# An attention and two-MLP kernel on one core: queues planned with another matmul cost, another rule for transfers, and unit tiles in groups of 4, 4, 8

## The chip, the core and the metric

One core of a Trainium2 chip runs the whole program. The metric is device time in microseconds (us). The engines are PE (matrix products), DVE (vector), ACT (activations), POOL (a second, slower vector engine) and SP, which only issues transfers. Each runs its own queue of instructions strictly in order and waits on semaphores where an operand is not ready.

## What is computed

A chunked attention (24 chunks of 32 queries, each against 56 neighbouring keys and 8 memory keys), then a first MLP whose activation is a rational function, then a second, gated MLP with four experts:

```python
# attention, per chunk: softmax(scale * q_c @ k_full.T) @ v_full
x = attn_out.transpose(0, 2, 1, 3).reshape(1536, 512)
# first MLP, w_in 512x2048, w_out 2048x512
h = x @ w_in
g = (a0 + a1*h + a2*h**2 + a3*h**3) / (1 + |b0|*|h| + |b1|*h**2 + 1e-6)
x = g @ w_out
# second MLP, E = 4 experts, w1 512x1024, w2 1024x512 each
out = sum_e p[:, e] * (relu(x @ w1[e]) @ w2[e])
```

## The kernel before

**Blocks and units.** The 1536 tokens are three blocks of 512. Attention is cut into 24 units (8 per block), each of 256 tokens and two heads. A unit has three pieces of PE work: the scores (L427, with a mask at L424), the transposes of the probabilities (L462), and the values (L479). Between them stand its softmax on DVE, POOL and ACT (L433 to L456) and the copies of the probabilities (L282). Its result goes to a tile of `x` (L548, L553).

**Splits.** Products run on pairs of a rounded value and its remainder, three products for each exact one (`PAIRS`). So everything that PE reads is split first: ACT copies the rounded half (L281), POOL or DVE subtracts to get the rest (L326).

**Steps of the first MLP.** The hidden size 2048 is cut into 16 unit tiles of 128. A step is one unit tile on one block, so there are 48 steps, numbered 0 to 47. I write A(i) for the first product of step i (12 matmuls, L569, into a bank of `h` or `att`) and B(i) for its second product (12 matmuls, L681, added up in the four `acc` banks). On PE, B(i) follows A(i+3) (`LAG` = 3). Between A(i) and B(i) stands the chain of the activation: ACT L633, L635, L672, L673; DVE L638, L642, then three instructions at L650, the last of which writes `ts<-ts,h` or `ts<-ts,att`; POOL L669; then ACT L281 and POOL L326, which write the split `g`. DVE has five instructions of this chain per step.

**Weights of the first MLP.** Each unit tile of weights comes as 64-bit words in two halves: half 0 for A, half 1 for B. A half is loaded (L349), converted by three DVE instructions (L352, L358, L364, here called a conversion), copied by ACT (L281) and split by POOL (L326, `w<-y,w`). Tiles live in the 10 buffers of `w`, which also hold the units' operands.

**Groups.** `GS = 4, 4, 4, 4` says that four unit tiles are run over all blocks before the next four, the blocks forward and backward in turn. This gives nine segments (block, first tile, end tile): (0,0,4) (1,0,4) (2,0,8) (1,4,8) (0,4,12) (1,8,12) (2,8,16) (1,12,16) (0,12,16). A segment ends after steps 3, 7, 15, 19, 27, 31, 39, 43 and 47. At its end the four `acc` banks are evicted: by ACT for the first segment of a block, by four DVE additions at L700 for the six others. The next segment's first B needs the freed banks.

**Second MLP.** Chunks of two unit tiles: direct products (L569), products on sums and differences of tiles (L795), second products (L928) evicted by DVE (L943, L945). The sums over blocks (`plan_sums_x`, L726) need two blocks to be finished.

**What sets the order.** All work is given to a planner as operations with costs (`Plan.add`), and `Plan.run` simulates the engines with those costs and emits the instructions in the order in which they came out. `MM` is the cost of one matmul of 512 columns, 0.2325. `Op.at` gives the moment at which an operation may start: its forerunners' ends plus a lag. Nominal PE times come from `tick`, which adds up costs in the order of the loops. Where the plan shows PE idle for over `FGAP`, `fill` adds matmuls on zeros (L294). These costs decide the order alone; on the chip every instruction waits for its real operands.

Of the kernel before, what the change touches and what calls it, by code (L numbers as in the profile page):

```python
# [26 lines left out]
NQ = 4  # L27
# [59 lines left out]
class Op:  # L87
# [4 lines left out]
        self.start = self.end = self.eng = None  # L92

    def at(self, e):
        return max((a.end + Plan.lag(a.eng, e) for a in self.after), default=0.0)


class Plan:
# [50 lines left out]
    def run(self):  # L149
        for o in self.ops:  # L150
            o.wait = len(o.after)
            o.start = o.end = None
            o.ready = 0.0
            for b in o.bufs:
                b.left, b.free = len(b.users), None
        live = {t: [] for t in BUFS}
        slots = {t: [] for t in BUFS}
        turn = {t: [] for t in BUFS}
        for o in sorted(self.ops, key=lambda o: (o.alap, o.n), reverse=True):
            for b in reversed(o.takes):  # L160
# [12 lines left out]
        for o in self.ops:  # L173
            if not o.wait:
                offer(o)
        done = 0
        while done < len(self.ops):
            best = None
            for e, lst in can.items():
                pick = None  # L180
                for o, c in lst:
                    if o.start is not None:
                        continue
                    t = max(free[e], o.at(e))
# [3 lines left out]
                    for b in o.takes:  # L188
                        if b.tag in live:
                            if turn[b.tag][-1] is not b:  # L190
# [3 lines left out]
                            if len(occ) >= BUFS[b.tag]:  # L194
                                times = sorted(x.free if x.free is not None else 1e9 for x in occ)
                                x = times[len(occ) - BUFS[b.tag]]
                                if x >= 1e9:
                                    ok = False
                                    break
                                t = max(t, x + 0.2)  # L200
                    if not ok:
                        continue
                    k = (t, o.alap)
                    if pick is None or k < pick[0]:
                        pick = (k, t, o, c)
                if pick is not None:
                    can[e] = [x for x in lst if x[0].start is None]
                    if best is None or pick[1] < best[0]:
# [43 lines left out]
def emit(ctx: ExitStack, tc: tile.TileContext, qk, v0, kv, q8, w64, w32, coef, prob, out):  # L252
# [140 lines left out]
    class Unit:  # L393
# [11 lines left out]
        def plan(self, t_scores, t_trans, t_values):  # L405
            u, blk, hp = self.u, self.blk, self.hp


            T = Buf("w", [128, 2048], F32)
            st = Buf("st", [128, 8], F32)  # L410
            P1, P2, P3 = self.psum_buf(), self.psum_buf(), self.psum_buf()
# [7 lines left out]
            def scores():  # L419
# [1 line left out]
                r = (blk * (BLK // UT) + self.half) % UPB  # L421
                edge = {0: 0, UPB - 1: NQ - 1}.get(r)
                if edge is not None:
                    PE.matmul(P1.ap[:, wide(edge)], ident_h, mask[:, min(edge, 1)], start=True, stop=False)  # L424
                for n in sorted(range(NQ), key=lambda n: n != edge):
                    for c in range(2):
                        PE.matmul(  # L427
                            P1.ap[64 * c : 64 * c + 64, wide(n)], q(c * NQ + n), k(c * NQ + n),
                            start=(n != edge), stop=True,
                        )  # L430

            def peaks():
                DVE.tensor_reduce(  # L433
                    out=nm(), in_=P1.ap[:, : NQ * KB].rearrange("p (n k) -> p n k", n=NQ),
                    axis=AX.X, op=ALU.max, negate=True,
                )

# [3 lines left out]
            def exps():  # L441
                for n in range(NQ):
                    ACT.activation(
                        k(n), P1.ap[:, n * KB : (n + 1) * KB], AF.Exp, scale=SCALE,
                        bias=nm()[:, n : n + 1], accum_out=sm()[:, n : n + 1],
                    )

# [12 lines left out]
            def trans():  # L460
                for n in range(2):
                    PE.transpose(  # L462
                        P2.ap[:, n * 128 : n * 128 + 128], T.ap[:, n * 128 : n * 128 + 128], ident
                    )

            def probs(j):
# [1 line left out]
                r = slice(64 * j, 64 * j + 64)  # L468
                copy(o_probs[j].eng)(
                    T.ap[r, 1024:1536].rearrange("p (g t x) -> p g t x", t=2, x=CH)[:, :, j],  # L470
                    P2.ap[r, :UT].rearrange("p (g x) -> p g x", x=CH),
                )

            def values():
                for n in range(2):
                    for c in range(2):
                        for h in range(2):
                            j = n * 4 + c * 2 + h
                            PE.matmul(  # L479
                                P3.ap[64 * h : 64 * h + 64, wide(c * 2 + n)],  # L480
                                v()[:, wide(j)], q(j), start=True, stop=True,
                            )

# [43 lines left out]
            o = add(  # L527
                [("POOL", 0.65)], norm3, [o], [st, T]
            )
            o2 = add([("PE", 0.22)], trans, [o], [T], [P2], key=t_trans)  # L530
            o_probs = [
                add(
                    [("ACT", 0.39), ("DVE", 0.45)] if blk == 0 else [("ACT", 0.39)],
# [1 line left out]
                )  # L535
                for j in range(2)
            ]
            o3 = add([("PE", 0.62)], values, [*o_probs, lv], [T], [P3], key=t_values)
            if u == FU:
                plan_warm(1, [o3], t_values + 0.1)  # L540
            ps = lambda: P3.ap[:, :UT]
            c = slice(self.half * UT, (self.half + 1) * UT)
            first = self.half == 0
            if first:
# [10 lines left out]
                ),  # L555
                [hi], [P3, X],
            )


    part, x2, acc, o_t = {}, {}, {}, {}  # L560
# [423 lines left out]

    todo = {}
    for b in range(1, NBLK):
        n = 2 * GS[0]
        for j in range(UB):
            at = b * n - UEND - (UB - 1 - j) * n / UB
            for part_, d in ((2, U2), (1, U1), (0, 0)):  # L990
                todo.setdefault(max(-1, round(at + d)), []).append((-part_, UB * b + j, part_))
    cost = (0.7, 0.22, 0.62)

    def attend(slot):
        for _, u, part_ in sorted(todo.pop(slot, [])):
            ut[u, part_] = tick(cost[part_])

    attend(-1)
    swaps = (GS[0], 2 * GS[0])
# [189 lines left out]
```

## Time and profile before

| what | value |
|---|---|
| time, median of 3 runs | 843.77 us (842.98 to 843.96) |
| the profiled execution | 843.32 us, of which its span is 841.5 us |
| PE busy | 819.9 us (97%) |
| DVE / POOL / ACT busy | 623.6 / 381.1 / 356.5 us |
| the chain that ended last | PE 65%, DVE 21%, ACT 5%, POOL 4%, DMA 2% |

A busy share counts an instruction as busy from its start to its (modelled) end, and a matmul that is held back can look long instead of late. So the distance from one start to the next tells more than the share. Times in the rows below count from the start of the span. "Idle before" is the time in which the engine stood still ahead of an instruction, with what ended the wait.

### The profile page before, as it was taken

What the parts mean: (1) busy time and instruction counts of PE and PEld (TensorE: products, weight loads), DVE (VectorE), ACT (ScalarE), POOL (GpSimd) and SP (SyncE); (2) the same over time, 40 slices, a digit from 0 to 9 for tenths busy, and PEclk for the clock granted to TensorE, in tenths of its full rate; (3) what the DMA queues carried; (4) which work ended last, traced back from release to release, by engine and by line L of the source; (5) the groups of instructions that cost most, each with busy time, mean ns of one, the idle gap of its engine ahead of it and who ended that gap; (6) DMA issues with size and microseconds to landing.
All of it is one profiled execution on the core that took longest, in us unless ns stands there. A gap on an engine that the chain in (4) does not pass through costs nothing.

```text
span 841.5 us, 11342 instructions
## 1 busy us (share of the span) xinstructions
PE 819.9 (97%) x4214; PEld 664.9 (79%) x4218; DVE 623.6 (74%) x929; ACT 356.5 (42%) x783; POOL 381.1 (45%) x350
## 2 busy tenths in 40 slices
PE   7889999999899998999999999999999999999998
PEld 4667778778788886788888888888888888888886
DVE  6988799999996679965766766766766765765754
ACT  6798886767666666430321321320320330330310
POOL 4797777877777797640321320330330330330300
PEclk9999999999999999999999999999999999999999
DMA  9976122212210100000101101101101101100003
GB/s 349 357 268 211 51 76 76 76 67 85 75 51 23 31 0 26 26 27 24 51 1 50 51 1 50 51 1 51 51 1 51 50 4 48 51 12 13 1 1 150
DMA packets 21911, 55.41 MB, mean 66 GB/s; under 512 B 3936, under 2 KB 3936, under 8 KB 21856
## 3 DMA queue, kind: packets, MB, share of 16 engines
q1 hardware_dynamic: 21856, 54.69, 19.0%
q8 instruction: 33, 0.54, 0.3%
q14 instruction: 22, 0.18, 0.1%
HBM read 51.54 MB, written 3.15 MB: 65 GB/s over the span
## 4 chain that ended last, share of the span: by engine, by line
PE 65%; DVE 21%; ACT 5%; POOL 4%; issue 2%; DMA 2%; SPq 0%; DVEq 0%; ACTq 0%; POOLq 0%
PE acc L928 30%; PE att L569 10%; PE h L795 10%; PE att L795 7%; DVE ts L650 5%; PE h L569 3%; PE acc L681 3%; DVE tm L638 2%; DVE tm L642 2%; DVE p L700 2%; DVE y L358 2%; DVE y L352 1%; DVE att L650 1%; DVE y L364 1%; DMA w<-kv 1%
## 5 line engine op out<-in xcount | busy, mean ns | idle before, releaser
L326 POOL TENSOR_TENSOR w<-stg,w 128x512 fp32r<-128x512 f32 x64 | 96.3, 1513 | 314.5 <-ACT w L281 314.5
L945 DVE SCALAR_TENSOR_TENSOR p<-acc,pr,p 128x512 f32<-128x512 f32 x180 | 135.2, 751 | 100.5 <-PE acc L928 100.5
L928 PE MATMUL acc<-w,g 128*128 128x512 f32 x768 | 177.5, 390 | 0.7 <-DVE p L943 0.6
L928 PEld LDWEIGHTS acc<-w,g 128*128 128x128 f32 x768 | 143.9, 188 | 31.6 <-DVE p L943 1.5
L681 PE MATMUL acc<-g,w 128*128 128x512 f32 x576 | 146.2, 398 | 4.1 <-DVE p L700 3.0
L569 PE MATMUL att<-x,w 128*128 128x512 f32 x624 | 147.8, 390 | 1.7 <-DVE ts L650 1.7
L569 PEld LDWEIGHTS att<-x,w 128*128 128x128 f32 x624 | 117.1, 188 | 26.3 <-DVE ts L650 2.1
L681 PEld LDWEIGHTS acc<-g,w 128*128 128x128 f32 x576 | 107.9, 190 | 31.2 <-DVE p L700 4.5
L281 ACT ACTIVATE ts<-h 128x512 f32<-128x512 f32 x15 | 9.0, 598 | 239.1 <-PE h L795 239.1
L569 PE MATMUL h<-x,w 128*128 128x512 f32 x384 | 96.5, 396 | 1.0 <-DVE ts L650 0.8
L928 PE MATMUL acc<-w,gb 128*128 128x512 f32 x384 | 89.6, 389 | 0.0
L569 PEld LDWEIGHTS h<-x,w 128*128 128x128 f32 x384 | 70.7, 188 | 16.8 <-DVE ts L650 1.3
L928 PEld LDWEIGHTS acc<-w,gb 128*128 128x128 f32 x384 | 72.1, 188 | 14.9
L326 POOL TENSOR_TENSOR g<-ts,g 128x512 fp32r<-128x512 f32 x48 | 66.7, 1390 | 26.7 <-ACT g L281 26.3
L669 POOL TENSOR_TENSOR ts<-ts,tu 128x512 f32<-128x512 f32 x48 | 63.8, 1329 | 12.8 <-ACT ts L658 10.9
L326 POOL TENSOR_TENSOR w<-y,w 128x512 fp32r<-128x512 f32 x36 | 49.9, 1386 | 8.3 <-ACT w L281 8.0
L281 ACT ACTIVATE g<-ts 128x512 fp32r<-128x512 f32 x48 | 30.3, 631 | 39.7 <-DVE ts L650 39.6
L795 PE MATMUL h<-x,w 128*128 128x512 f32 x180 | 45.7, 389 | 0.0
L795 PE MATMUL att<-x,w 128*128 128x512 f32 x180 | 45.7, 389 | 0.0
L795 PE MATMUL h<-w 128*128 128x512 f32 x180 | 45.7, 389 | 0.0
L795 PEld LDWEIGHTS h<-x,w 128*128 128x128 f32 x180 | 33.8, 188 | 7.0
L795 PEld LDWEIGHTS att<-x,w 128*128 128x128 f32 x180 | 33.8, 188 | 7.0
(122 smaller groups left out, 1168.3 us busy)
## 6 DMA issues: line engine op xcount, KB each, us to landing
stg<-w SPq DMA_DIRECT2D x64, 512.0 KB, 3.5
w<-kv SPq DMA_DIRECT2D x32, 256.0 KB, 5.2
w<-q SPq DMA_DIRECT2D x16, 256.0 KB, 4.8
w<-qk SPq DMA_DIRECT2D x8, 400.0 KB, 6.3
out<-p SPq DMA_DIRECT2D x12, 256.0 KB, 2.0
w<-v SPq DMA_DIRECT2D x8, 256.0 KB, 6.7
pr<-prob SPq DMA_DIRECT2D x1, 24.0 KB, 3.7
cf<-coef SPq DMA_DIRECT2D x1, 3.0 KB, 6.0
```

The costliest lines, as they stand in the source:

```text
L281: return lambda o, i: ACT.activation(o, i, AF.Copy)
L326: engines[op.eng].tensor_tensor(out=dst[:, 1], in0=src, in1=dst[:, 0].bitcast(F32), op=ALU.subtract)
L358: DVE.scalar_tensor_tensor(out=y.ap, in0=words(1), scalar=-(1 << 30), in1=y.ap, op0=ALU.bitwise_and, op1=ALU.bitwise_or,)
L569: PE.matmul(s.h.ap, wt[w].ap[:, 0, a, k * 128 : (k + 1) * 128], xs[k].ap[:, b], start=(k == 0 and n == 0), stop=(k == KT - 1 and n == 2),)
L638: [("DVE", 0.6)], lambda: DVE.tensor_tensor(out=m.ap, in0=m.ap, in1=h.ap, op=ALU.mult), [li], [h, m]
L642: lambda: DVE.scalar_tensor_tensor(out=m.ap, in0=m.ap, scalar=A1, in1=h.ap, op0=ALU.add, op1=ALU.mult),
L650: lambda: DVE.scalar_tensor_tensor(out=out.ap, in0=in0.ap, scalar=scalar, in1=in1.ap, op0=op0, op1=op1),
L669: lambda: POOL.tensor_tensor(out=s.ap, in0=s.ap, in1=u.ap, op=ALU.mult), [ln], [s, u],
L681: PE.matmul(ps, wt[f].ap[:, 1, a, d * 128 : (d + 1) * 128], g.ap[:, b], start=start, stop=stop)
L795: PE.matmul(ps.ap, left(a, k), right(b, k), start=k == 0 and n == 0, stop=k == 1 and n == 2,)
L928: PE.matmul(ps.ap, gs[j][0].ap[:, a, d * 128 : d * 128 + 128], wt[f].ap[:, 1, b], start=j == 0 and n == 0, stop=j == 1 and n == 2,)
L945: DVE.scalar_tensor_tensor(out=y, in0=ps.ap, scalar=p, in1=y, op0=ALU.mult, op1=ALU.add)
```

## The change

- `MM` becomes 0.2267. The costs of the attention's PE pieces become 0.85, 0.25 and 0.8 (`PARTS`; before 0.75, 0.22 and 0.62).
- In the plan, an SP operation that follows another SP operation may start 0.5 after the other's start (`Op.at`); before, it waited for the landing and a lag of 0.9. So a unit's `v` may be issued right behind its keys and queries.
- `GS` becomes 4, 4, 8. The segments are (0,0,4) (1,0,4) (2,0,8) (1,4,8) (0,4,16) (1,8,16) (2,8,16): seven, ending after steps 3, 7, 15, 19, 31, 39 and 47. The last blocks to end now come in the order 0, 1, 2 (before 2, 1, 0), so block 0 is finished after step 31.
- Attention pieces are planned as generators; PSUM banks of units 8 to 11 are taken in the order of the pieces. Merging pieces into one PE operation is written down, but `MERGED` = 9 is beyond the last block, so nothing is merged.

```diff
-MM = 0.2325
+MM = 0.2267
-UEND, U1, U2 = 3, 2, 3
+UEND, UD, MERGED = 3, (0, 2, 3), 9
+PARTS, GROUPED, SWITCH = (0.85, 0.25, 0.8), (0.5, 0.22, 0.45), 0.3
-GS = 4, 4, 4, 4
+GS = 4, 4, 8
     def at(self, e):
-        return max((a.end + Plan.lag(a.eng, e) for a in self.after), default=0.0)
+        return max((a.start + 0.5 if a.eng == e == "SP" else a.end + Plan.lag(a.eng, e) for a in self.after), default=0.0)
...
-            o1 = add([("PE", 0.75)], scores, [*ready, o_mask, o_ident], [T], [P1], key=t_scores)
+            o1 = yield 0, scores, [*ready, o_mask, o_ident], [T]
+            P1 = self.at[0][0]
...
+    def cost_of(parts):
+        return PARTS[parts[0]] if len(parts) == 1 else SWITCH + sum(GROUPED[n] for n in parts)
+
+    def attend_ops(wants, key):
...
+        o = add([("PE", cost_of([w[2][0] for w in wants]))], go, after, uses, takes, key=key)
+        return [gen.send(o) for _, gen, _ in wants]
...
-    for u in units:
-        u.plan(*(ut[u.u, j] for j in range(3)))
+    for u in units[:UB]:
+        gen = u.parts()
+        want = next(gen)
+        for j in range(3):
+            (want,) = attend_ops([(u, gen, want)], ut[u.u, j])
+    gens, wants = {u.u: u.parts() for u in units[UB:]}, {}
```

**First place: SP at the start of the program.** `qk` and `v` are the operands of the units of block 0, `kv` and `q` those of later units, `stg` a half of a weight tile of the first MLP. Before:

```order
L502 DMA w<-qk 128x800 x7
L509 DMA w<-v 128x512
L502 DMA w<-qk 128x800
L509 DMA w<-v 128x512
L349 DMA stg<-w 128x512
L509 DMA w<-v 128x512
L505 DMA w<-kv 128x512
L506 DMA w<-q 128x512
L509 DMA w<-v 128x512
```

After, from the same place:

```order
L508 DMA w<-qk 128x800 x5
L515 DMA w<-v 128x512
L508 DMA w<-qk 128x800
L515 DMA w<-v 128x512
L508 DMA w<-qk 128x800 x2
L515 DMA w<-v 128x512 x6
L351 DMA stg<-w 128x512
L511 DMA w<-kv 128x512
L512 DMA w<-q 128x512
```

All eight `v` of block 0 now stand ahead of the first weight half; before, six of them stood behind it, with later units' operands and two more weight halves in between. For later units, too, `v` now follows its keys: the `v` of units 10 and 11 stood behind five weight halves (tiles 0 to 3, and half 1 of tile 0) and now stand behind three.

**Second place: DVE after step 27.** `y<-stg` are conversions, `tm`, `h`, `att` and `ts` belong to the chain of steps 27 to 29, `p<-acc,p` is an eviction. Before:

```order
L650 SCALAR_TENSOR_TENSOR ts<-ts,h 128x512
L638 TENSOR_TENSOR tm<-tm,h 128x512
L642 SCALAR_TENSOR_TENSOR tm<-tm,cf,h 128x512
L364 SCALAR_TENSOR_TENSOR y<-stg,y 128x512
L352 TENSOR_SCALAR y<-stg 128x512
L650 SCALAR_TENSOR_TENSOR ts<-ts,cf,h 128x512
L650 SCALAR_TENSOR_TENSOR h<-tm,cf,h 128x512
L700 TENSOR_TENSOR p<-acc,p 128x512 x4
L650 SCALAR_TENSOR_TENSOR ts<-ts,h 128x512
```

After, from the end of step 28 to that of step 29:

```order
L687 SCALAR_TENSOR_TENSOR ts<-ts,h 128x512
L679 SCALAR_TENSOR_TENSOR tm<-tm,cf,att 128x512
L360 SCALAR_TENSOR_TENSOR y<-stg,y 128x512
L354 TENSOR_SCALAR y<-stg 128x512
L366 SCALAR_TENSOR_TENSOR y<-stg,y 128x512
L360 SCALAR_TENSOR_TENSOR y<-stg,y 128x512
L687 SCALAR_TENSOR_TENSOR ts<-ts,cf,att 128x512
L687 SCALAR_TENSOR_TENSOR att<-tm,cf,att 128x512
L675 TENSOR_TENSOR tm<-tm,att 128x512
L687 SCALAR_TENSOR_TENSOR ts<-ts,att 128x512
```

The four evictions are gone, since no segment ends there. The conversions are those of tiles 12 to 15 in both, but of other halves: the L366 here ends the conversion of half 1 of tile 12, which B(28) reads; before, tile 12 was first used by step 36. In both kernels 18 conversions stand between the last chain instruction of step 9 and that of step 32.

**Third place: DVE at the end of the first MLP**, from the last chain instruction of step 47 to the last four evictions. `g<-` are splits for the second MLP, `y<-p`, `tu` and `w` belong to the sums of blocks and weights. Before:

```order
L650 SCALAR_TENSOR_TENSOR ts<-ts,att 128x512
L726 TENSOR_TENSOR tu<-tu,stg 128x256
L726 TENSOR_TENSOR y<-p,y 128x512
L907 SCALAR_TENSOR_TENSOR g<-h,g 128x512
L726 TENSOR_TENSOR tu<-stg,tu 128x256
L726 TENSOR_TENSOR y<-p,y 128x512
L907 SCALAR_TENSOR_TENSOR g<-att,g 128x512
L326 TENSOR_TENSOR w<-tu,w 128x512
L326 TENSOR_TENSOR w<-y,w 128x512
L726 TENSOR_TENSOR y<-p,y 128x512
L907 SCALAR_TENSOR_TENSOR g<-h,g 128x512
L700 TENSOR_TENSOR p<-acc,p 128x512 x4
```

After:

```order
L687 SCALAR_TENSOR_TENSOR ts<-ts,att 128x512
L328 TENSOR_TENSOR w<-y,w 128x512
L944 SCALAR_TENSOR_TENSOR g<-h,g 128x512
L763 TENSOR_TENSOR y<-p,y 128x512
L944 SCALAR_TENSOR_TENSOR g<-att,g 128x512
L944 SCALAR_TENSOR_TENSOR g<-h,g 128x512
L737 TENSOR_TENSOR p<-acc,p 128x512 x4
```

Ten instructions stood ahead of the evictions; five do now. Of the other five three have moved ahead of step 47's chain and two to POOL.

## Rows read from the trace of the kernel before

**Rows 1.** The page, busy time, share of the span, instructions.
```profile
PE 819.9 (97%) x4214; PEld 664.9 (79%) x4218; DVE 623.6 (74%) x929; ACT 356.5 (42%) x783; POOL 381.1 (45%) x350
```

**Rows 2.** Windows: stretch, length, busy time by engine, granted clock, DMA share, GB/s.
```profile
0.00:27.30 27.30, 19.93 (x319) 13.88 (x321) 19.53 (x59) 16.84 (x84) 12.76 (x34) 1.00 0.95 351
27.30:60.00 32.70, 28.91 (x315) 20.59 (x313) 28.02 (x55) 29.23 (x107) 29.23 (x38) 1.00 0.84 299
...
119.00:250.00 131.00, 127.08 (x541) 102.12 (x540) 123.84 (x176) 88.69 (x148) 100.12 (x77) 0.99 0.21 73
250.00:320.00 70.00, 70.00 (x310) 57.87 (x310) 49.55 (x73) 45.97 (x78) 53.48 (x47) 1.00 0.06 16
320.00:353.00 33.00, 30.25 (x128) 23.27 (x126) 32.55 (x43) 17.45 (x31) 26.68 (x20) 1.00 0.10 32
353.00:837.90 484.90, 484.75 (x2136) 400.93 (x2136) 320.65 (x443) 107.66 (x192) 114.29 (x87) 1.00 0.10 33
```

**Rows 3.** Pieces of the chain that ended last: start, length, what.
```profile
30.23 6.28 DMA w<-kv
...
378.11 5.44 PE att L569 x24
```

**Rows 4.** Timeline of PE around B(28): start, length, line, count, idle before.
```profile
226.31 2.20 PE L569 MATMUL att<-x,w 128*128 128x512 f32 x9
230.58 5.34 PE L681 MATMUL acc<-g,w 128*128 128x512 f32 x12 [2.07 <-DVE p L700]
235.76 0.62 PE L569 MATMUL h<-x,w 128*128 128x512 f32 x2
```

**Rows 5.** Timeline of DVE in the same place.
```profile
228.05 0.41 DVE L352 TENSOR_SCALAR y<-stg 128x512 int32<-128x512 int32 x1
...
229.75 2.48 DVE L700 TENSOR_TENSOR p<-acc,p 128x512 f32<-128x512 f32 x4
232.14 0.68 DVE L650 SCALAR_TENSOR_TENSOR ts<-ts,h 128x512 f32<-128x512 f32 x1
```

**Rows 6.** Windows in the same place, for the granted clock.
```profile
228.40:230.60 2.20, 0.13 (x2) 0.05 (x1) 2.20 (x5) 2.20 (x4) 1.27 (x1) 1.00 0.63 194
...
233.00:235.80 2.80, 2.80 (x10) 2.19 (x9) 2.80 (x5) 2.39 (x5) 2.24 (x2) 0.62 0.02 6
```

**Rows 7.** Timeline of PE from B(44) into the second MLP.
```profile
320.13 0.39 PE L681 MATMUL acc<-g,w 128*128 128x512 f32 x1
...
324.16 2.89 PE L569 MATMUL h<-x,w 128*128 128x512 f32 x12
326.89 2.88 PE L681 MATMUL acc<-g,w 128*128 128x512 f32 x12
331.46 3.02 PE L569 MATMUL att<-x,w 128*128 128x512 f32 x12 [1.68 <-DVE ts L650]
...
345.20 7.18 PE L928 MATMUL acc<-w,g 128*128 128x512 f32 x30
353.01 1.20 PE L928 MATMUL acc<-w,g 128*128 128x512 f32 x4 [0.64 <-DVE p L943]
```

**Rows 8.** Timeline of POOL: the split of the first weight half.
```profile
23.47 1.27 POOL L326 TENSOR_TENSOR w<-y,w 128x512 fp32r<-128x512 f32 x1 [0.42 <-ACT w L281]
```

**Rows 9.** Timeline of PE: A(0) and one matmul of A(1).
```profile
27.32 3.26 PE L569 MATMUL h<-x,w 128*128 128x512 f32 x13
```

**Rows 10.** Timeline of DVE: end of step 47's chain, and the last evictions.
```profile
334.95 0.69 DVE L650 SCALAR_TENSOR_TENSOR ts<-ts,att 128x512 f32<-128x512 f32 x1
...
344.37 2.48 DVE L700 TENSOR_TENSOR p<-acc,p 128x512 f32<-128x512 f32 x4
```

**Rows 11.** Lines, DVE, 119 to 250: conversions; busy us, mean ns, idle before.
```profile
L358 DVE SCALAR_TENSOR_TENSOR y<-stg,y 128x512 int32<-128x512 int32 x17 | 18.2, 1073 | 0.0
L364 DVE SCALAR_TENSOR_TENSOR y<-stg,y 128x512 int32<-128x512 int32 x18 | 15.8, 880 | 0.0
L352 DVE TENSOR_SCALAR y<-stg 128x512 int32<-128x512 int32 x17 | 14.2, 832 | 2.4 <-POOL w L326 2.4
```

More of the change, by code (lines that the diff above doesn't have):

```diff
@@ L187, in run @@
                     ok = True
-                    for b in o.takes:
+                    for i, b in enumerate(o.takes):
                         if b.tag in live:
-                            if turn[b.tag][-1] is not b:
+                            n = sum(x.tag == b.tag for x in o.takes[:i])
+                            if turn[b.tag][-1 - n] is not b:
                                 ok = False
@@ L193, in run @@
                             occ = live[b.tag]
-                            if len(occ) >= BUFS[b.tag]:
+                            if len(occ) + n >= BUFS[b.tag]:
                                 times = sorted(x.free if x.free is not None else 1e9 for x in occ)
-                                x = times[len(occ) - BUFS[b.tag]]
+                                x = times[len(occ) + n - BUFS[b.tag]]
                                 if x >= 1e9:
@@ L403, in psum_buf, with parts @@
             return bank((["att"] * 2 + ["acc"] * 4)[Unit.turn])
-        def plan(self, t_scores, t_trans, t_values):
+        def parts(self):
             u, blk, hp = self.u, self.blk, self.hp
+            self.at = {}
+            at = lambda part_, n: self.at[part_][0].ap[:, self.at[part_][1] : self.at[part_][1] + n]
+            p1, p2, p3 = lambda: at(0, UT), lambda: at(1, UT), lambda: at(2, UT)
             T = Buf("w", [128, 2048], F32)
             st = Buf("st", [128, 8], F32)
-            P1, P2, P3 = self.psum_buf(), self.psum_buf(), self.psum_buf()
             wide = lambda j: slice(j * 64, j * 64 + 64)
@@ L423, in scores @@
                 if edge is not None:
-                    PE.matmul(P1.ap[:, wide(edge)], ident_h, mask[:, min(edge, 1)], start=True, stop=False)
+                    PE.matmul(p1()[:, wide(edge)], ident_h, mask[:, min(edge, 1)], start=True, stop=False)
                 for n in sorted(range(NQ), key=lambda n: n != edge):
@@ L427, in scores @@
                         PE.matmul(
-                            P1.ap[64 * c : 64 * c + 64, wide(n)], q(c * NQ + n), k(c * NQ + n),
+                            p1()[64 * c : 64 * c + 64, wide(n)], q(c * NQ + n), k(c * NQ + n),
                             start=(n != edge), stop=True,
@@ L433, in peaks @@
                 DVE.tensor_reduce(
-                    out=nm(), in_=P1.ap[:, : NQ * KB].rearrange("p (n k) -> p n k", n=NQ),
+                    out=nm(), in_=p1().rearrange("p (n k) -> p n k", n=NQ),
                     axis=AX.X, op=ALU.max, negate=True,
@@ L443, in exps @@
                     ACT.activation(
-                        k(n), P1.ap[:, n * KB : (n + 1) * KB], AF.Exp, scale=SCALE,
+                        k(n), p1()[:, n * KB : (n + 1) * KB], AF.Exp, scale=SCALE,
                         bias=nm()[:, n : n + 1], accum_out=sm()[:, n : n + 1],
@@ L462, in trans @@
                     PE.transpose(
-                        P2.ap[:, n * 128 : n * 128 + 128], T.ap[:, n * 128 : n * 128 + 128], ident
+                        p2()[:, n * 128 : n * 128 + 128], T.ap[:, n * 128 : n * 128 + 128], ident
                     )
@@ L470, in probs @@
                     T.ap[r, 1024:1536].rearrange("p (g t x) -> p g t x", t=2, x=CH)[:, :, j],
-                    P2.ap[r, :UT].rearrange("p (g x) -> p g x", x=CH),
+                    p2()[r].rearrange("p (g x) -> p g x", x=CH),
                 )
@@ L479, in values @@
                             PE.matmul(
-                                P3.ap[64 * h : 64 * h + 64, wide(c * 2 + n)],
+                                p3()[64 * h : 64 * h + 64, wide(c * 2 + n)],
                                 v()[:, wide(j)], q(j), start=True, stop=True,
@@ L529, in plan @@
             )
-            o2 = add([("PE", 0.22)], trans, [o], [T], [P2], key=t_trans)
+            o2 = yield 1, trans, [o], [T]
+            P2 = self.at[1][0]
             o_probs = [
@@ L537, in plan @@
             ]
-            o3 = add([("PE", 0.62)], values, [*o_probs, lv], [T], [P3], key=t_values)
+            o3 = yield 2, values, [*o_probs, lv], [T]
+            P3 = self.at[2][0]
             if u == FU:
-                plan_warm(1, [o3], t_values + 0.1)
-            ps = lambda: P3.ap[:, :UT]
+                plan_warm(1, [o3], o3.key + 0.1)
+            ps = p3
             c = slice(self.half * UT, (self.half + 1) * UT)
@@ L557, in plan, with go @@
             )
+            yield
+    def cost_of(parts):
+        return PARTS[parts[0]] if len(parts) == 1 else SWITCH + sum(GROUPED[n] for n in parts)
+    def attend_ops(wants, key):
+        takes, fns, after, uses = [], [], [], []
+        shared = None
+        for unit, gen, (part_, fn, need, use) in wants:
+            if part_ == 0 or shared is None:
+                b = unit.psum_buf()
+                takes.append(b)
+                if part_:
+                    shared = b
+            else:
+                b = shared
+            unit.at[part_] = b, (UT if part_ == 2 and len(wants) > 1 else 0)
+            fns.append(fn)
+            after += need
+            uses += use
+        def go():
+            for fn in fns:
+                fn()
+        o = add([("PE", cost_of([w[2][0] for w in wants]))], go, after, uses, takes, key=key)
+        return [gen.send(o) for _, gen, _ in wants]
     part, x2, acc, o_t = {}, {}, {}, {}
@@ L986, in emit @@
     for b in range(1, NBLK):
[L987 to L992, printed above, removed]
+        for j in range(UB + UD[2]):
+            at = max(-1, round(b * 2 * GS[0] - UEND - (UB - 1 - j) * 2 * GS[0] / UB))
+            group = [(UB * b + j - UD[n], n) for n in (2, 1, 0) if 0 <= j - UD[n] < UB]
+            todo.setdefault(at, []).extend([group] if b >= MERGED else [[x] for x in group])
+    groups = []
     def attend(slot):
-        for _, u, part_ in sorted(todo.pop(slot, [])):
-            ut[u, part_] = tick(cost[part_])
+        for x in todo.pop(slot, []):
+            groups.append((x, tick(cost_of([n for _, n in x]))))
     attend(-1)
@@ L1040, in emit @@
     o_coef = add([("DVE", 0.2)], set_coef, [o_coef])
-    for u in units:
-        u.plan(*(ut[u.u, j] for j in range(3)))
+    for u in units[:UB]:
[4 more added lines that the diff above has]
+    gens, wants = {u.u: u.parts() for u in units[UB:]}, {}
+    for x, key in groups:
+        for u, n in x:
+            if n == 0:
+                wants[u] = next(gens[u])
+        for (u, _), want in zip(x, attend_ops([(units[u], gens[u], wants[u]) for u, _ in x], key)):
+            wants[u] = want
     for blk in range(NBLK):
```

## Prediction

> **What bounds the kernel now.** I read the page first: PE is busy for 97% of the span [rows 1], so PE sets the end, and the question is where it loses time. The windows by stage answer that [rows 2]. From 353 on, through the whole second MLP, PE is busy for 484.75 of 484.9 us, and 24 matmuls take 5.44 us there [rows 3], 0.2267 each. The new `MM` is that number. No order of DVE, ACT or POOL can shorten this part, and its order on PE is the same in both kernels but for block numbers. The change can only move what lies before 353.
>
> There PE loses in three places. In the first 60 us it is idle for 7.4 and 3.8 us, while the DMA share is 0.95 and 0.84 [rows 2]: it waits for operands. From 119 to 250 DVE is busy for 123.84 of 131 us, from 320 to 353 for 32.55 of 33, and from 250 to 320, where DVE has 20 us to spare, PE has no gap at all [rows 2]. So in the middle and at the end of the first MLP DVE is a second bound, and PE loses time where DVE's queue is late.
>
> The busy share hides some of it, so I count from start to start. The worst place is B(28), the first product of a segment [rows 4]. The 9 matmuls from 226.31 should end 2.04 later, at 228.35; B(28) starts at 230.58, so 2.23 are lost. Its 12 matmuls last until 235.76, 5.18 instead of 2.72, another 2.46; together 4.69. The wait ended with DVE's evictions, which stand at 229.75 to 232.14 [rows 5], behind conversions and chain instructions. The granted clock was 0.62 of full speed in 233 to 235.8, so part of these matmuls ran at the lower level, 1.2 GHz, after an engine that had done almost nothing from 228.4 to 230.6 [rows 6]. At the end of the stage the same reading gives three losses [rows 7]: B(44) takes 4.03 from 320.13 to 324.16 instead of 2.72 (1.31); the next A should follow B(45) at 329.61 and starts at 331.46 (1.85); and in the second MLP's first products 30 matmuls from 345.20 should end at 352.00, while the next starts at 353.01 after a wait of 0.64 for an eviction (I count 0.8 as lost).
>
> **The new matmul cost, the unit costs, the generators.** They add no instruction. The matmuls, conversions and splits are the same; 15 matmuls on zeros stand in the order instead of 20, all within PE's gaps. Their worth is in the order alone, so they go into the terms below. PE's work before 353 is not changed by them: zero, hidden by nothing.
>
> **The start.** The new rule for transfers lets all `v` of block 0 go ahead of the first weight half. Six of them, 1.5 MB, now precede it; at 351 GB/s [rows 2] that half lands up to 4.4 us later. Against this, the chain passed through the `v` of a later unit from 30.23 on for 6.28 us [rows 3]. That `v` stood behind five weight halves and now stands behind three: 1.0 MB less, 3.4 us at 299 GB/s. What could be won is capped by ACT, busy for 29.23 of 32.7 us from 27.3 to 60 [rows 2]: 3.5 us. So the bounds are a loss of 4.4 and a gain of 3.5. POOL had split the first half by 23.47 + 1.27 = 24.74 [rows 8] and A(0) began at 27.32 [rows 9], so 2.6 of the 4.4 cost nothing; I stay nearer to the gain and take **1.5**.
>
> **The middle.** Without a segment end after step 27, four evictions leave DVE's queue: 229.75 to 232.14, **2.4** us [rows 5]. The 18 conversions from step 9 to step 32 stay. On an engine that is busy for 95% of this stretch [rows 2], time taken out should come out of PE's lateness. The bounds are 0 (the lateness shows somewhere else) and 4.69 (the whole loss at B(28) goes, clock included). I take the 2.4 of the evictions, since DVE stays late and something has to wait for it. What is late next are the conversions of tiles 12 to 15: they were needed from step 36 on and now from step 28.
>
> **The end.** The evictions after step 43 go as well: B(44)'s 1.31 is gone [rows 7]. Between step 47's chain and the last evictions DVE needed 344.37 - 334.95 = 9.42 us for ten instructions [rows 10]; five are left, so the last evictions come some 4.7 us earlier against that chain, and the 0.8 ahead of 353 goes. Ahead of step 47's end the four evictions are replaced by three more instructions of the sums, about even, so of the 1.85 I take half. Block 0 is finished after step 31, and its splits find DVE and POOL idle between 250 and 320 [rows 2]. Sum 1.31 + 0.8 + 0.9 = **3.0**, bounds 1 and 3.96. The cover is that free stretch; without it the splits would cost what they do now.
>
> **Sum.** 1.5 + 2.4 + 3.0 = 6.9. The profiled execution took 843.32, so 836.4; it lay 0.45 below the median, so **836.9** in a measurement of medians.
>
> **Rivals.** *The lock.* A conversion's first instruction took 0.41 at 228.05 [rows 5], yet 0.83 on average in this stretch, the others 1.07 and 0.88 [rows 11]. Something holds them up, and POOL is busy for 100.12 us beside them [rows 2]. If conversions and POOL take turns on one resource, they need 48.2 + 100.1 = 148 us, waits included, of 131, and evictions, which read PSUM, free nothing of it. Then the middle gives nothing: 843.77 - 1.5 - 3.0 = 839.3. For it: the stretched instructions. Against: POOL is idle for 31 us there, and the wait at B(28) ended with an eviction, not with a conversion. The Trainium skill (SBUF — State Buffer, Who interferes with whom) says that a DVE instruction with two SBUF inputs, or in a two-port mode, and a POOL instruction that reads SBUF exclude each other, the second blocked until the first has ended; by that rule this rival holds, and the trace agrees as far as the stretched conversions go.
>
> *Lost at the start.* The first weight half is what A(0) really waits for: 4.4 lost instead of 1.5 won, 843.77 + 4.4 - 2.4 - 3.0 = 842.8. For it: the DMA share of 0.95 [rows 2]; an earlier transfer only delays another. Against: it was ready 2.6 us early [rows 8, 9].
>
> *Late tiles, slower than before.* B(28) to B(31) each read half 1 of a tile whose conversion DVE ends just after the chain of the same step. If PE waits there as long as at B(28) before, 2.23 us [rows 4], the clock falls again; at 0.62 over 2.8 us [rows 6] that is at least 1.1 more, at most the 2.46, so 4.0 a stall. From two stalls on (8.0 against 6.9) the kernel is slower; with three of four it is 836.9 + 12 = 848.9. For it: conversions of 2.8 us (1.07 + 0.88 + 0.83) and a chain already fill most of a step of 5.44 us. Against: they did so before, with evictions on top.
>
> *Everything goes.* 3.5 at the start, 4.69 and 3.96: 12.15, 831.6. *Nothing happens,* the replanned queues wait as long in other places: 843.8.
>
> **Chances.** Forecast 0.48, the lock 0.15, lost at the start 0.12, late tiles 0.10, everything 0.10, nothing 0.05. A measurement of this kernel can tell about 0.2%, 1.7 us. Faster by more than that, below 842.1: 0.48 + 0.15 + 0.10 = 0.73. Within it: 0.12 + 0.05 = 0.17. Slower: 0.10. The range reaches from "everything" to "lost at the start", 831.5 to 843.0; late tiles and nothing are left out, 0.15.
>
> **What would show it.** The start: A(0) no later than 27.3 and B(0) earlier. The middle: no wait for DVE evictions at B(28), the granted clock at 1.00 through 220 to 240, and B(31) earlier by the first two terms. The lock: conversions whose mean grows, and B(31) earlier by the start alone. Late tiles: PE waiting for POOL's `w<-y,w` at B(28) to B(31). The end: B(44) lasting 2.7, and no wait of PE from 320 on. A second MLP that takes anything but 485 us would prove my first paragraph wrong.

## The result, and the profile after

The changed kernel takes 835.02 us (median of 4 runs, 834.40 to 836.09); the kernel before took 843.52 beside it (842.98 to 843.96). The ratio is 0.9899, 95% interval 0.9885 to 0.9914: faster by 8.5 us, where 6.9 was forecast. The profiled execution took 835.54, its span is 833.4.

The page, first row, to compare with [rows 1]:

```profile
PE 816.5 (98%) x4208; PEld 663.6 (80%) x4213; DVE 613.8 (74%) x913; ACT 361.9 (43%) x792; POOL 381.3 (46%) x349
```

Windows by stage of the changed kernel, as [rows 2] (stretch, length, busy time of PE, PEld, DVE, ACT and POOL, granted clock, DMA share, GB/s):

```profile
60.00:119.00 59.00, 58.26 (x469) 45.10 (x468) 47.48 (x87) 50.23 (x146) 42.41 (x51) 1.00 0.35 118
119.00:250.00 131.00, 129.34 (x561) 104.42 (x559) 122.84 (x172) 92.22 (x154) 101.55 (x78) 1.00 0.22 72
250.00:320.00 70.00, 69.72 (x304) 56.63 (x303) 53.36 (x78) 49.83 (x86) 60.58 (x50) 1.00 0.06 16
320.00:345.00 25.00, 25.00 (x112) 20.69 (x111) 24.24 (x32) 12.62 (x23) 19.92 (x16) 1.00 0.13 42
345.00:829.60 484.60, 484.60 (x2138) 400.92 (x2137) 319.27 (x441) 107.04 (x191) 113.71 (x86) 1.00 0.10 33
```

The second MLP is as full as before, and the end of the first MLP is now full too. From 119 to 250 PE still loses a little, and DVE is nearly as busy there as before. The timeline of PE (start, length, line, count, idle before) answers [rows 4], [rows 7] and [rows 9]; line numbers are 37 higher than before for L569 and L681:

```profile
25.67 3.05 PE L606 MATMUL h<-x,w 128*128 128x512 f32 x12
...
226.85 1.20 PE L718 MATMUL acc<-g,w 128*128 128x512 f32 x4
228.23 2.10 PE L718 MATMUL acc<-g,w 128*128 128x512 f32 x8 [0.18 <-POOL w L328]
...
238.44 1.21 PE L718 MATMUL acc<-g,w 128*128 128x512 f32 x4
239.82 2.12 PE L718 MATMUL acc<-g,w 128*128 128x512 f32 x8 [0.16 <-POOL w L328]
...
249.93 3.79 PE L718 MATMUL acc<-g,w 128*128 128x512 f32 x12
253.56 2.88 PE L606 MATMUL h<-x,w 128*128 128x512 f32 x12
...
316.72 2.88 PE L718 MATMUL acc<-g,w 128*128 128x512 f32 x12
...
330.32 2.88 PE L606 MATMUL h<-x,w 128*128 128x512 f32 x12
...
338.48 6.74 PE L965 MATMUL acc<-w,g 128*128 128x512 f32 x29
```

A(0) begins at 25.67 (27.32 before). B(28) begins at 226.85, only 0.24 late, with no wait for an eviction; in B(28) and B(30) PE waits shortly for POOL's split of the weights (`w`), 0.6 each from start to start. B(32) lasts 3.63 instead of 2.72, held by the evictions of step 31. B(44), at 316.72, lasts 2.72 (1.31 less), and nothing waits behind it. The timeline of DVE at the end of the stage, as [rows 10]:

```profile
329.58 0.69 DVE L687 SCALAR_TENSOR_TENSOR ts<-ts,att 128x512 f32<-128x512 f32 x1
...
334.95 2.47 DVE L737 TENSOR_TENSOR p<-acc,p 128x512 f32<-128x512 f32 x4
```

Five instructions and 5.37 us lie between the chain of step 47 and the last evictions, where ten and 9.42 lay.

**Where the time came from.** I follow four points of PE's queue through both traces, in us:

| point | before | after | won so far | won in the stretch |
|---|---|---|---|---|
| A(0) begins | 27.32 | 25.67 | 1.65 | |
| A(12) begins (all attention done) | 118.97 | 119.25 | -0.28 | -0.28 |
| B(33) begins | 260.26 | 256.28 | 3.98 | 4.26 |
| the last product begins | 837.40 | 829.21 | 8.19 | 4.21 |

The last column counts from the start of the span for A(12). The "last product" is the last matmul of the program. One shift of work must be taken out of these figures: three matmuls of later steps (`att<-x,w`) stand behind A(12) before and ahead of it after (15 from 110.13 on before, 18 from 109.73 on after). They are 0.68 of PE's work that the stretch A(12) to B(33) no longer holds. At equal work, as I call it below, the start gave 0.40, the middle 3.58, the end 4.21.

### The profile page after: what moved, and what is told of

It reads as the page before. It is cut to its first block, busy times and chain, and to the rows that moved or that the text cites. A ratio compares the mean times of both kernels' runs of the same rounds, so it can differ in the third digit from the quotient of the medians.

```text
span 833.4 us, 11348 instructions
## 1 busy us (share of the span) xinstructions
PE 816.5 (98%) x4208; PEld 663.6 (80%) x4213; DVE 613.8 (74%) x913; ACT 361.9 (43%) x792; POOL 381.3 (46%) x349
## 4 chain that ended last, share of the span: by engine, by line
PE 71%; DVE 14%; ACT 5%; DMA 3%; POOL 3%; issue 2%; SPq 1%; DVEq 0%; ACTq 0%; POOLq 0%
PE acc L965 31%; PE att L606 12%; PE h L832 10%; PE att L832 7%; PE acc L718 5%; PE h L606 4%; DVE ts L687 3%; DVE y L354 2%; DVE y L360 2%; DVE tm L679 2%; DVE tm L675 2%; POOL ts L706 1%; DMA w<-q 1%; DVE y L366 1%; DMA w<-kv 1%
## 5 line engine op out<-in xcount | busy, mean ns | idle before, releaser
L718 PE MATMUL acc<-g,w 128*128 128x512 f32 x576 | 144.0, 394 | 1.8 <-ACT g L283 1.1
L606 PEld LDWEIGHTS att<-x,w 128*128 128x128 f32 x624 | 117.1, 188 | 24.3
L606 PEld LDWEIGHTS h<-x,w 128*128 128x128 f32 x384 | 70.4, 188 | 16.5 <-DVE ts L687 1.5
L328 POOL TENSOR_TENSOR g<-ts,g 128x512 fp32r<-128x512 f32 x48 | 69.6, 1452 | 12.2 <-ACT g L283 11.9
L706 POOL TENSOR_TENSOR ts<-ts,tu 128x512 f32<-128x512 f32 x48 | 65.7, 1370 | 10.9 <-ACT ts L695 7.2
L328 POOL TENSOR_TENSOR w<-y,w 128x512 fp32r<-128x512 f32 x35 | 45.5, 1303 | 18.6 <-ACT w L283 18.0
L283 ACT ACTIVATE w<-tu 128x512 fp32r<-128x512 f32 x30 | 19.0, 633 | 48.9 <-POOL tu L763 43.2
L832 PEld LDWEIGHTS h<-w 128*128 128x128 f32 x180 | 33.8, 188 | 7.0
```

Of the source, the lines that this page charges most:

```text
L283: return lambda o, i: ACT.activation(o, i, AF.Copy)
L328: engines[op.eng].tensor_tensor(out=dst[:, 1], in0=src, in1=dst[:, 0].bitcast(F32), op=ALU.subtract)
L606: PE.matmul(s.h.ap, wt[w].ap[:, 0, a, k * 128 : (k + 1) * 128], xs[k].ap[:, b], start=(k == 0 and n == 0), stop=(k == KT - 1 and n == 2),)
L706: lambda: POOL.tensor_tensor(out=s.ap, in0=s.ap, in1=u.ap, op=ALU.mult), [ln], [s, u],
L718: PE.matmul(ps, wt[f].ap[:, 1, a, d * 128 : (d + 1) * 128], g.ap[:, b], start=start, stop=stop)
L832: PE.matmul(ps.ap, left(a, k), right(b, k), start=k == 0 and n == 0, stop=k == 1 and n == 2,)
```

## Experiments

All ratios are against the kernel before, run on the same chip beside each kernel. From every profile (one execution of each kernel) I read the same points, and "PE's loss" in a stretch: for each matmul of 512 columns, the time to the next start beyond 0.227 us (where it is over 0.03 more), summed. Names that begin with b_ are the kernel before with one part of the change, those with a_ the changed kernel with one part taken back or altered, those with x_ the changed kernel with other planned costs.

| kernel | median us | ratio (95%) | A(0) | A(12) | last product | PE's loss 119-256 | 256-355 |
|---|---|---|---|---|---|---|---|
| before | 843.5 | 1 | 27.32 | 118.97 | 837.40 | 8.55 | 4.58 |
| after | 835.02 | 0.9899 (0.9885-0.9914) | 25.67 | 119.25 | 829.21 | 4.90 | 0.57 |
| b_gs | 838.32 | 0.9944 (0.9930-0.9957) | 27.29 | 119.00 | 832.15 | 8.00 | 0 |
| a_gs | 838.82 | 0.9948 (0.9935-0.9960) | 26.37 | 119.46 | 832.87 | 5.68 | 3.04 |
| b_sp | 843.10 | 0.9994 (0.9986-1.0003) | 26.18 | 118.70 | 836.28 | 8.96 | 3.11 |
| a_sp | 835.51 | 0.9909 (0.9895-0.9924) | 20.75 | 120.49 | 829.33 | 3.80 | 0 |
| b_mm | 840.91 | 0.9967 (0.9956-0.9977) | 28.39 | 124.61 | 834.82 | 4.05 | 3.03 |
| a_mm | 836.62 | 0.9924 (0.9911-0.9936) | 24.89 | 117.69 | 829.43 | 5.93 | 0 |
| x_pool | 834.58 | 0.9894 (0.9880-0.9907) | 24.72 | 121.32 | 828.39 | 3.23 | 0 |
| x_b | 827.74 | 0.9811 (0.9798-0.9825) | 25.62 | 117.12 | 821.78 | 0 | 0.15 |
| x_b4444 | 828.16 | 0.9816 (0.9801-0.9831) | 26.41 | 117.90 | 822.43 | 0 | 0 |
| x_b448 | 831.48 | 0.9859 (0.9842-0.9875) | 24.85 | 116.37 | 824.54 | 3.48 | 0 |
| a_466 | 834.52 | 0.9894 (0.9880-0.9909) | 24.99 | 118.66 | 828.62 | 3.82 | 1.73 |

**The parts apart.** First the groups alone (b_gs) and everything but the groups (a_gs). In both PE's and SP's queues keep their order.

```diff
b_gs, against before:
-GS = 4, 4, 4, 4
+GS = 4, 4, 8
a_gs, against after:
-GS = 4, 4, 8
+GS = 4, 4, 4, 4
```

> The kernel before with the groups 4, 4, 8 and nothing else; PE's and SP's queues keep their order, only DVE, ACT and POOL change. If the eight evictions that leave DVE's queue are what the middle and the end gain by, this kernel takes nearly the whole gain: B(28) without a wait for evictions (up to 4.7), B(44) of 2.7 and no wait at 329.6 and 352 (up to 4.0), 835 to 837. If the new costs and the new rule for transfers make the gain, by an order in which conversions and chains hinder each other less, it gives at most the end, 840 or more.

> The changed kernel with the groups back at 4, 4, 4, 4: the new costs and the new rule for transfers are all that is left of the change. If the groups make the gain, 842.5 to 844, with the waits for evictions at B(20), B(28), B(44) back. If costs and rule make it, 837 to 840.

Neither came out as one theory had it: each half of the change is worth about 4.5 us, 4.7 (843.5 x 0.0056) and 4.4, and together they are worth 8.5. The groups clear the end (4.58 to 0) and next to nothing of the middle (8.55 to 8.00). In b_gs B(28) no longer waits, and B(29) begins at 233.82, 4.68 earlier than before (238.50), the whole loss of [rows 4]. But here is PE's timeline of b_gs at B(29), B(31) and B(32):

```profile
233.82 2.88 PE L681 MATMUL acc<-g,w 128*128 128x512 f32 x12
...
244.77 0.50 PE L681 MATMUL acc<-g,w 128*128 128x512 f32 x1
246.40 2.80 PE L681 MATMUL acc<-g,w 128*128 128x512 f32 x11 [1.13 <-POOL w L326]
249.04 2.88 PE L569 MATMUL att<-x,w 128*128 128x512 f32 x12
253.21 4.03 PE L681 MATMUL acc<-g,w 128*128 128x512 f32 x12 [1.28 <-ACT g L281]
```

B(31) lasts 1.6 too long, 1.4 of it for the split of its weights (`w`); then B(32) starts 1.4 late for a chain (`g`) and loses 1.2 more inside; at B(33) only 0.46 is left of the 4.68. This is the rival of the late tiles, in the kernel with the groups alone. All costs of the planner together with the rule for transfers, with the old groups (a_gs), take 2.9 out of the middle and 1.5 out of the end.

**The rule for transfers**, alone and taken back:

```diff
b_sp, against before (a_sp: the reverse, against after):
-        return max((a.end + Plan.lag(a.eng, e) for a in self.after), default=0.0)
+        return max((a.start + 0.5 if a.eng == e == "SP" else a.end + Plan.lag(a.eng, e) for a in self.after), default=0.0)
```

> The kernel before with the new rule for transfers and nothing else. A(0) should begin about 1.6 earlier, as in the changed kernel. If the front is bound by ACT, POOL and the order of the transfers together, the 1.6 is gone by A(12) (118.97 before, 119.25 in the changed kernel) and the time is that of before, 843 to 844.5. If the gain at A(0) stays and was lost in the changed kernel to the new costs, A(12) begins at 117.5 and the time is 842.

> The changed kernel with the old rule for transfers: a unit's values wait for the landing of its keys again. If the start is worth the 1.5 of the sum, 836 to 837.5, with A(0) at 27 or later and A(12) later than 119.25. If ACT, POOL and DVE bound the front whatever the transfers do (the rule alone moved the kernel before by 0.06%), within 1 of the changed kernel, 834 to 836.

The rule is worth nothing that can be measured: 0.9994 (0.9986 to 1.0003) alone, and without it the change is 0.9909 instead of 0.9899, with intervals that overlap. A(0) is no measure of the front: in a_sp it begins at 20.75, five us before the changed kernel's, and A(12) comes 1.2 later (1.9 at equal work). Behind A(12) a_sp loses 1.7 less (3.80 against 5.47), although a late tile is back at B(31), where PE waits 1.47 for POOL's `w`. So in the changed kernel the rule does bring the front forward, and what it brings is lost again behind it; in b_sp the front does not gain.

**The cost of a matmul**, alone and taken back:

```diff
b_mm, against before (a_mm: the reverse, against after):
-MM = 0.2325
+MM = 0.2267
```

> The kernel before with 0.2267 for a matmul and nothing else. It issues no other work and plans the same segments. If the cost only renames the same order, within 1 us of before, 842.5 to 844.5. If the planner's finer timing is what takes DVE's lateness out of the middle, B(20) and B(28) lose less and it takes 838 to 841.

> The changed kernel with the cost of a matmul back at 0.2325; groups, unit costs and the rule for transfers stay. With the groups alone PE lost 4.2 on the late tile of B(31) and B(32). If the matmul cost is what keeps the new groups from running into late tiles, these waits are back here between 220 and 256 and the time is 838 to 840. If the new unit costs or the rule for transfers do that, this kernel is within 1 of the changed one, 834 to 836.

A number that only the planner sees is worth 2.8 us alone (its seven runs spread from 839.37 to 841.93). From 119 to 256 PE loses half as much (8.55 to 4.05), but A(12) comes 5.64 later, 3.6 at equal work, and 2.3 of that is a wait for a DVE chain (`ts`) that ends at 119.01, in the table's front but of the middle's kind. Counted with it, PE loses 6.4 there and not 4.05. Taken back it costs 1.6 to 2.1 us (836.62 against 835.02, ratio 0.9924 against 0.9899), between the two expectations: the late tiles don't return, but PE waits for the evictions at B(20) instead, and some 1.6 of the loss there is the lower clock behind these waits (last section). The same work in another order waits in another place.

**The costs tuned further.** In x_pool POOL's planned costs are 4% higher. In x_b the whole ratio is moved: a matmul is planned 3% cheaper than it is, ACT and POOL 3% dearer than in the changed kernel (DVE 1% cheaper, 0.16 instead of 0.15 between engines), and the groups are 4, 6, 6.

```diff
x_pool, against after:
+SC = {'POOL': 1.04}
...
+        ways = [(e, c * SC.get(e, 1.0)) for e, c in ways]
x_b, against after:
-MM = 0.2267
+MM = 0.2197
...
-GS = 4, 4, 8
+SC = {'ACT': 1.033, 'POOL': 1.032, 'DVE': 0.991}
+GS = 4, 6, 6
...
+        ways = [(e, c * SC.get(e, 1.0)) for e, c in ways]
...
-        return 0.2 if a == "PE" else 0.15
+        return 0.2 if a == "PE" else 0.16
```

> The changed kernel with POOL's planned costs 4% higher (1.28 instead of 1.23 for 512 columns; the trace shows 1.27 to 1.30). No instruction is added. If planned costs below the real ones are what puts conversions and splits too late or too early in the queues, the order made with the real cost loses less after 119: 829 to 833. If the order of the changed kernel is already as good as the costs can make it, within 1.5 of it, 833.5 to 836.5.

> The changed kernel with groups 4, 6, 6, a matmul at 0.2197, ACT and POOL 3% dearer, DVE 1% cheaper, and 0.16 instead of 0.15 between engines: PE is planned faster against the others than it is, so that chains come ahead of conversions, and the last group has six tiles to bring in instead of eight. If late tiles and late chains are an effect of the planner's ratio of costs, PE loses next to nothing from 119 on (5.5 in the changed kernel): 828 to 831. If the ratio only moves the waits about, 834 to 837.

x_pool is the changed kernel again, within the noise: a cost nearer to the trace is not by itself a better order. It lost 1.7 less in the middle, and A(12) came 2.1 later (1.4 at equal work). x_b is 15.9 us faster than before (843.5 x 0.0189) and 7.3 faster than the changed kernel. It loses nothing from 119 to 250. To see what of it is the costs and what the groups, three kernels part them:

```diff
x_b4444, against x_b:
-GS = 4, 6, 6
+GS = 4, 4, 4, 4
x_b448, against x_b:
-GS = 4, 6, 6
+GS = 4, 4, 8
a_466, against after:
-GS = 4, 4, 8
+GS = 4, 6, 6
```

> The costs of the fastest kernel so far (a matmul at 0.2197, ACT and POOL 3% dearer, DVE 1% cheaper, 0.16 between engines) with the old groups 4, 4, 4, 4, so with all 24 evictions and nine segments. If DVE is a second bound in the middle and the eight evictions are what it lacks, PE waits at B(20), B(28) or B(32) again and loses 3 to 5 between 119 and 256: 833 to 837. If only the order of conversions and chains counts, PE loses nothing there even with all evictions, and only the end still pays for the late third blocks (3 to 5): 829 to 832.

> The same costs with the groups of the change, 4, 4, 8. If the ratio of costs makes the gain, 828 to 831, with the eight tiles of the last group as the one place that may still wait (B(28) to B(31), up to 3). If 4, 6, 6 makes it, as the changed kernel, 834 to 836.

> The changed kernel with the groups 4, 6, 6 and nothing else. If the groups make the gain of the fastest kernel, 827 to 830. If the ratio of costs makes it, within 2 of the changed kernel, 833 to 837.

It is the costs. With the old groups and all 24 evictions, x_b4444 takes 828.16, as x_b does. Groups 4, 6, 6 without the costs give 834.52, as the changed kernel. Which of the altered costs does it was not told apart. Windows of x_b4444:

```profile
119.00:250.00 131.00, 131.00 (x579) 108.31 (x578) 127.19 (x181) 94.76 (x158) 100.37 (x78) 1.00 0.19 63
250.00:320.00 70.00, 70.00 (x311) 57.96 (x310) 57.45 (x85) 49.28 (x85) 64.82 (x55) 1.00 0.12 31
320.00:353.00 33.00, 33.00 (x147) 27.32 (x146) 24.92 (x32) 12.88 (x23) 18.95 (x15) 1.00 0.10 32
```

DVE is busy for 127.19 of 131 us, more than the 123.84 of [rows 2], and PE has no gap. B(28) shows why. Timeline of PE, then of DVE, in x_b4444:

```profile
217.41 2.88 PE L720 MATMUL acc<-g,w 128*128 128x512 f32 x12
220.13 2.88 PE L608 MATMUL att<-x,w 128*128 128x512 f32 x12
222.85 2.91 PE L720 MATMUL acc<-g,w 128*128 128x512 f32 x12
```

```profile
219.68 0.42 DVE L356 TENSOR_SCALAR y<-stg 128x512 int32<-128x512 int32 x1
220.02 1.27 DVE L739 TENSOR_TENSOR p<-acc,p 128x512 f32<-128x512 f32 x2
221.40 0.75 DVE L689 SCALAR_TENSOR_TENSOR ts<-ts,cf,h 128x512 f32<-128x512 f32 x1
222.06 1.28 DVE L739 TENSOR_TENSOR p<-acc,p 128x512 f32<-128x512 f32 x2
```

B(27) gives way to A(31) at 220.13. The evictions run at 220.02 and 222.06, two and two, and B(28) starts at 222.85 on time. The kernel before, in the same place, timeline of PE and of DVE (the evictions themselves are in [rows 5]):

```profile
222.91 2.88 PE L681 MATMUL acc<-g,w 128*128 128x512 f32 x12
225.63 2.88 PE L569 MATMUL att<-x,w 128*128 128x512 f32 x12
```

```profile
226.18 0.75 DVE L642 SCALAR_TENSOR_TENSOR tm<-tm,cf,h 128x512 f32<-128x512 f32 x1
226.84 1.28 DVE L364 SCALAR_TENSOR_TENSOR y<-stg,y 128x512 int32<-128x512 int32 x1
228.05 0.41 DVE L352 TENSOR_SCALAR y<-stg 128x512 int32<-128x512 int32 x1
228.43 0.75 DVE L650 SCALAR_TENSOR_TENSOR ts<-ts,cf,h 128x512 f32<-128x512 f32 x1
229.09 0.75 DVE L650 SCALAR_TENSOR_TENSOR h<-tm,cf,h 128x512 f32<-128x512 f32 x1
```

There B(27) gave way at 225.63 and the evictions came at 229.75: five instructions, two of them conversions for a later step, stood ahead of them. The wait at B(28) was not the length of the evictions but their place in the queue.

The groups of the change are the one choice that the good costs don't cure: x_b448 is 3.3 us behind x_b4444. PE's timeline of x_b448 at B(28):

```profile
223.76 1.19 PE L720 MATMUL acc<-g,w 128*128 128x512 f32 x4 [1.60 <-ACT w L285]
225.47 2.11 PE L720 MATMUL acc<-g,w 128*128 128x512 f32 x8 [0.53 <-POOL w L330]
```

These are late tiles again: half 1 of tile 12, from step 36 moved to step 28.

**The lock.** In lock1 the order is the changed kernel's, and most of the square term's work on POOL is left out:

```diff
lock1, against after (W = 8 for steps 9 to 31, else 512):
-                lambda: POOL.tensor_tensor(out=s.ap, in0=s.ap, in1=u.ap, op=ALU.mult), [ln], [s, u],
+                lambda: POOL.tensor_tensor(
+                    out=s.ap[:, :W], in0=s.ap[:, :W], in1=u.ap[:, :W], op=ALU.mult
+                ), [ln], [s, u],
```

> The changed kernel with POOL's product of the activation (the square term, ts<-ts,tu) done on 8 of 512 columns in steps 9 to 31: 23 instructions of 1.30 fall to about 0.1, some 28 of POOL's 101 us between 119 and 250, and the output is not the reference's. The order of all queues stays. If conversions and POOL exclude each other, the conversions beside them shrink towards 0.41, 0.66 and 0.68 (means of 1.11, 0.88 and 0.90 to below 0.95, 0.80 and 0.80), and the 3.8 that PE still loses from 119 to 256 mostly go: 831 to 833. If what stretches the conversions is something else (their source's layout, the transfers), their means stay within 0.05 and only the chain is shorter by the product: 833 to 835.

It took 829.22 (0.9836, 0.9822 to 0.9849), less than either expectation, PE lost nothing after 119, and two of the three conversions shrank to 0.77 and 0.75, while the first stayed at 1.11. That conversions and POOL hold each other up is seen better in the changed kernel's own timelines, DVE first and then POOL:

```profile
224.02 1.51 DVE L354 TENSOR_SCALAR y<-stg 128x512 int32<-128x512 int32 x1
```

```profile
223.58 1.67 POOL L328 TENSOR_TENSOR g<-ts,g 128x512 fp32r<-128x512 f32 x1 [0.15 <-ACT g L283]
```

A conversion that takes 0.41 undisturbed [rows 5] ended at 225.53, 0.28 after POOL's split ended at 225.25. In the changed kernel 22 of the 49 conversions from 119 to 250 are stretched (the first over 0.5, the others over 0.75), and each of the 22 ends 0.28 to 0.55 after a POOL instruction does; of the other 27 only two do. In lock1, 15 are left, each ending in the same way. The planner already counts on this: in `Plan.run`, operations on DVE with `lock=True`, the conversions among them, never overlap POOL's. But the lock doesn't bound the middle. The lines of DVE in x_b, 119 to 250, to compare with [rows 11]:

```profile
L362 DVE SCALAR_TENSOR_TENSOR y<-stg,y 128x512 int32<-128x512 int32 x16 | 17.6, 1099 | 0.1
L368 DVE SCALAR_TENSOR_TENSOR y<-stg,y 128x512 int32<-128x512 int32 x17 | 15.9, 934 | 0.0
L356 DVE TENSOR_SCALAR y<-stg 128x512 int32<-128x512 int32 x16 | 13.5, 848 | 0.0
```

About the same means as before (1.07, 0.88, 0.83), and PE waits for none of it. So lock1 tells what taking some 28 us of POOL's work away gives, and not that the lock was the cause: its chain became shorter too, and the two are not told apart.

## Why the prediction was right, and where it was not

The time, the sign and the place of the gain were right: nothing in the second MLP (485 us in both), all of it before. The sum was right for partly wrong reasons, since its errors partly cancel: at equal work -1.1 at the start, +1.2 in the middle, +1.2 at the end.

- **What bounds the kernel.** PE as the bound, and the three places of its loss, hold. "DVE is a second bound" in the middle does not: DVE at 127.19 of 131 us let PE run without a gap in x_b4444. Its busy share showed a full queue; the loss came from what stood ahead of what. The Trainium skill (Perfetto Trace Analysis, Identifying the Most-Contended Engine) takes occupancy as the sign of the engine to work on first; here the measurement differs, since the stretch in which DVE is busier is the one without a loss.
- **The new matmul cost, the unit costs.** No work is added, as said. The step that failed is the next one: their worth was booked into the terms, and the terms were then sized from the groups alone. Alone, the matmul cost takes 2.8 us off (b_mm), and all but the groups takes 4.4 off (a_gs).
- **The start, 1.5.** Measured -0.28, or 0.40 at equal work. A(0) came earlier, as the prediction wanted to see, and so did B(0), by 5.5; neither decides the front. The wait for the later unit's `v` on the chain of waits was booked as time of the whole program, which it was not: the rule alone gives 0.9994 (b_sp), and in the changed kernel the 1.9 that it gives at A(12) is lost behind it (a_sp). What binds the front was not told apart. Before, DVE, ACT and POOL are busy for 28.02, 29.23 and 29.23 of the 32.7 us behind A(0) [rows 2], but other costs moved A(12) from 119.25 to 116.37 (x_b448), so 2 to 3 us of the front are order as well.
- **The middle, 2.4.** Measured 4.26 (3.58 at equal work), inside its bounds, but by another cause. Four evictions taken out of the queue gave the upper bound, 4.68, at B(29), and 4.2 of it was lost again within four steps, to a late tile and to a late chain and evictions behind it (b_gs). "Time taken out should come out of PE's lateness" was the false sentence: PE's lateness was one wait for one place in the queue. The changed kernel is spared most of the late tiles, by the new costs and the rule together: a_mm, without the matmul cost, has none of these waits, and a_sp, without the rule, has the one at B(31) again. The unit costs were not tried alone.
- **The end, 3.0.** Measured 4.21, and here the cause is as said: the groups alone take 4.58 down to 0. I had counted the wait of 1.85 by half; it went whole, with 0.13 behind it, and the 0.8 ahead of 353 went with 0.67 of small delays around it; 0.57 was lost anew at step 39's evictions. The groups are enough for that, not needed: x_b4444 loses nothing there with the old ones.
- **Rivals.** Late tiles, with a chance of 0.10, is what the groups alone run into: 1.6 at the tile itself, 2.6 behind it. In the changed kernel 1.2 of it is left, at B(28) and B(30). The lock agrees with the traces as a mechanism and falls as a bound: the Trainium skill (SBUF — State Buffer, Who interferes with whom) lets a DVE instruction and a POOL instruction of these kinds exclude each other, the ends of all 22 stretched conversions agree, and x_b and x_b4444 lose nothing by it. Lost at the start and everything goes didn't happen.

## What to carry over

A second engine that is busy for 95% beside a full PE is not a bound until an order has been tried in which what PE waits for stands first: read at the wait which instructions stood ahead of the late one, and whom they serve. Where a planner sets the order, its ratio of costs is a parameter of its own: with a matmul planned 3% cheaper than it is, and ACT and POOL 3% dearer, the rest of the change with the old groups gained nearly twice what the change gained (828.16), without one eviction less. And a saving in a queue should be followed for some steps behind the place where it appears, since the next late operand can take it back.

## What the runs showed of the hardware

The clock did not fall for every wait of that kind. Before B(28) PE had waited for 2.23, and the granted clock went down to 1.2 GHz for much of what followed [rows 6]. In b_gs B(31) waited for 1.4 and B(32) again for 1.4; windows of b_gs show the clock at 1.00 (2.4 GHz) through a microsecond without a matmul and behind it:

```profile
252.00:253.00 1.00, 0.00 (x0) 0.00 (x0) 1.00 (x3) 0.51 (x1) 0.95 (x1) 1.00 0.00 0
253.00:255.00 2.00, 1.56 (x4) 0.65 (x4) 2.00 (x5) 2.00 (x5) 1.80 (x2) 1.00 0.00 0
255.00:256.00 1.00, 1.00 (x5) 0.82 (x6) 0.96 (x2) 0.52 (x1) 1.00 (x2) 1.00 0.00 0
```

The 1.1 to 2.46 that the rival of the late tiles added to each wait for the clock was therefore not paid there. Nor does the length of one wait tell: in x_b448 PE lost 1.76 ahead of B(28) and the clock stayed at 1.00, while in a_mm it fell after PE had lost 0.78 ahead of B(20) and 1.03 inside it. Window of a_mm behind these two:

```profile
186.00:187.50 1.50, 1.50 (x5) 1.21 (x4) 1.50 (x3) 0.83 (x2) 0.20 (x1) 0.50 0.00 0
```

And the fall behind B(28) cost the kernel before little at its end. It is not in every execution: four of the kernel before have a mean granted clock of 1.000, and they took 843.13 to 843.42, 0 to 0.51 below the medians of the measurements that they belong to (843.13 to 843.69). In the profiled execution the six matmuls at the lower level lost 1.1. Where the rest of that goes was not traced.
